# First batch's attention in two halves of its query rows, with layer 1 of the first 256 tokens between them

## The chip, the cores and the metric

The kernel runs on one core of a Trainium2 chip. A time is the device time of one execution in microseconds (us). Engines: TensorE (PE, its weight loads PEld), VectorE (DVE), ScalarE (ACT), GpSimd (POOL), and SyncE (SP), whose queue issues nearly all DMAs here. Each engine takes its instructions in the order of the program and waits at one that is not ready.

## What is computed

Inputs and outputs are float32 (the layer 1 to 3 weights float64). Attention with a block-causal mask over 8 batches, 8 heads, 576 tokens and head size 64, a gated double layer, and a top-1 mixture of 8 experts:

```python
scores = scale * np.matmul(q, k.transpose(0, 1, 3, 2))
mask = (pos[:, None] // 64) >= (pos[None, :] // 64)
attn = softmax(np.where(mask, scores, -1e9))
x = np.matmul(attn, v)               # to (4608 tokens, 512)
h = ((x @ w1) * (x @ w2)) @ w3       # 512 -> 1024 -> 1024
x2 = h @ w_out                       # 1024 -> 512
# gate logits of x2, one expert of 8 per token, relu(x2 @ w1[e]) @ w2[e], times the gate
```

## The kernel before

Nearly all matmuls are made of a high and a low float32r part of each operand (`split`: ACT writes the high part as a copy, DVE or POOL the low part as a subtraction), so that three matmuls, or two where one operand's parts are stacked, give one float32 product.

**Attention** (`attention`, a generator) goes through 32 pairs of heads, four pairs to a batch, nine steps to a pair. A step is a tile of 128 query rows: (hd, i) is head hd, rows 128 i onwards, with 128 (i + 1) key columns; (0, 4) is the last 64 rows of both heads. A step's stages are in successive iterations: scores on PE, one later the row maximum on DVE (L288), two later the exponential on ACT (L296), three later the normalization by DVE and POOL (L303), five later the transposes on PE, six later their evacuation by ACT and DVE to `pth` and `ptl`, seven later the product with V on PE (L350), eight later its output and split into `xph` and `xpl`. While a pair is in work the next one's inputs are prepared: ACT writes the high parts of q, K and V (L178, L189, L199), POOL the low parts (L183, L194, L204). The raw tiles are single buffers, so a load waits on SP until both engines have read the one before.

**The float32 route.** For pairs 0 to 2 (`N_RAW`) q and K are not split: `score_f32` multiplies them as float32, at four passes of PE.

**Layer 1** (`layer1(b)`) multiplies batch b's 576 tokens with w1 and w2: 8 feature blocks, 2 halves of 288 tokens, 2 weights, 12 matmuls each, so 384 matmuls a batch. It can start when all four pairs of the batch are through, that is 8 iterations behind the pair's last step.

**The weight decoder** (`decoder`) turns 16 chunks of float64 words of w1 and w2 into parts: for each chunk two copies on ACT (L113, L104), three integer instructions on DVE (L120, L121, L123), one subtraction on POOL (L105). Twelve chunks go ahead of layer 1, four beside it.

**The order** comes from one loop: attention yields after each half iteration, and `filler` (decoder, then layer 1 of batches 0 to 6) is advanced by a debt, 600 ns of estimated work a yield until batch 0 is ready, then 2335 ns an iteration less the attention's own PE cost. Behind attention come layer 1 of the last batch, the fold of w3 with w_out, routing and the experts.

Of the kernel before, what the change touches and what calls it, by code (L numbers as in the profile page):

```python
# [19 lines left out]

N_RAW, N_DEC = 3, 12
# [25 lines left out]
def tile_moe_stack(ctx: ExitStack, tc: tile.TileContext, qd, kd, vd, w1, w2, w3t, wo, wg,  # L47
                   e1, e2, c_id, c_msk, c_tri, c_row, c_cst, out):
    nc = tc.nc
# [97 lines left out]

    def attention(sa):
# [12 lines left out]
        def load(p, what):  # L161
            if p >= NP:
                return
            shape, src = {"q": ([128, 2, 640], qd), "k": ([128, 2, 576], kd), "v": ([128, 5, 2, 64], vd)}[what]
# [6 lines left out]
            raws[p, what] = t = raw.tile(shape, F32, tag=what + "r", name=what + "r")  # L171
            nc.sync.dma_start(out=t, in_=src[p])

        def prep_q1(p, h):
            if h == 0:
                ops.setdefault(p, {})
                ops[p]["X"] = opd.tile([128, 2, 640], F32R, tag="X", name="X")
            nc.scalar.activation(out=ops[p]["X"][:, h], in_=raws[p, "q"][:, h], func=AF.Copy)  # L178

        def prep_q2(p, h):  # L180
            q_, x = raws[p, "q"], ops[p]["X"]
            os_ = slice(64 - 64 * h, 128 - 64 * h)
            nc.gpsimd.tensor_tensor(out=x[os_, h], in0=q_[os_, h], in1=x.bitcast(F32)[os_, h],  # L183
                                                          op=ALU.subtract)

        def prep_k1(p, h):
            if h == 0:
                ops[p]["K1"] = opd.tile([128, 2, 576], F32R, tag="K1", name="K1")
            nc.scalar.activation(out=ops[p]["K1"][:, h], in_=raws[p, "k"][:, h], func=AF.Copy)  # L189

        def prep_k2(p, e):

            ops[p]["K2", e] = t = opd.tile([128, 576], F32R, tag="K2", name="K2", bufs=3)
            nc.gpsimd.tensor_tensor(out=t, in0=raws[p, "k"][:, e], in1=ops[p]["K1"].bitcast(F32)[:, e], op=ALU.subtract)  # L194

        def prep_v1(p):
            vv = opd.tile([128, 5, 2, 128], F32R, tag="VV", name="VV")
            ops.setdefault(p, {})
            nc.scalar.activation(out=vv[:, :, :, 0:64], in_=raws[p, "v"], func=AF.Copy)  # L199
            ops[p]["VV"] = vv  # L200

        def prep_v2(p):
            vv, v_ = ops[p]["VV"], raws[p, "v"]
            nc.gpsimd.tensor_tensor(out=vv[:, :, :, 64:128], in0=v_, in1=vv.bitcast(F32)[:, :, :, 0:64],  # L204
                                    op=ALU.subtract)

        def split_only(f):
            def go(p):
                if p >= N_RAW:
                    f(p)  # L210
            return go

        def then(f, what):
            def go(p):
                f(p)
                if what == "v" or p >= N_RAW:
                    load(p + 1, what)
            return go

        def early(p):  # L220
            if p + 1 < N_RAW:
                load(p + 1, "q")
                load(p + 1, "k")

        def first_split(p):
            if p == N_RAW - 2:
                load(N_RAW, "q")
                load(N_RAW, "k")

        prep_at = [(0, 0, then(prep_v2, "v")), (0, 1, split_only(lambda p: prep_q1(p, 0))),  # L230
                   (1, 1, split_only(lambda p: prep_q2(p, 0))), (1, 1, split_only(lambda p: prep_q1(p, 1))),
                   (2, 1, then(split_only(lambda p: prep_q2(p, 1)), "q")), (3, 1, split_only(lambda p: prep_k1(p, 0))),
                   (4, 1, split_only(lambda p: prep_k2(p, 0))), (4, 1, split_only(lambda p: prep_k1(p, 1))),
                   (6, 1, then(split_only(lambda p: prep_k2(p, 1)), "k")), (8, 1, prep_v1)]

        def score_f32(n, p, hd, i):
            X, K = ops[p]["X"].bitcast(F32), ops[p]["K1"].bitcast(F32)
            if i < 4:
                w_ = 128 * (i + 1)
                st = ps_s.tile([128, 512], F32, tag="s", name="s")  # L240
                nc.tensor.matmul(st[:, :w_], lhsT=X[0:64, hd, 128 * i:128 * i + 128], rhs=K[0:64, hd, :w_], start=True, stop=True)
                jobs[n] = dict(parts=[(st[:, :w_], 0, w_)], n=w_)
                return 4 * w_ / 2.4
            parts = []
            for c in range(2):
                st = ps_s.tile([128, 512], F32, tag="s", name="s")
                sl = slice(288 * c, 288 * c + 288)
                for h in range(2):
                    nc.tensor.matmul(st[:, :288], lhsT=X[0:64, h, 512:640], rhs=K[0:64, h, sl], start=(h == 0), stop=(h == 1))
# [863 lines left out]
```

## Time and profile before

| | |
|---|---|
| three runs | 1587.75 us median, 1581.91 to 1590.41 |
| profiled execution | 1582.65 us, span 1580.9 us |
| busy PE, DVE, ACT, POOL | 1516.8, 976.9, 883.8, 744.0 us |
| instructions | 28995 |

Busy time is the time in which an engine has an instruction in work; on PE matmuls overlap, so the start to start distance of two of them is what a matmul costs. In a timeline row the bracket at the end is the engine's idle time before the instruction and what ended it. In a group row the number behind the comma is the mean duration of one in ns.

### The profile page before, as it was taken

To read this page: it belongs to the slowest core of one execution; us is meant where nothing else is said; L and a number is where in the kernel's file an instruction comes from. 1 tells how busy PE (TensorE), PEld (TensorE's weight loads), DVE (VectorE), ACT (ScalarE), POOL (GpSimd) and SP (SyncE) were. 2 spreads that over 40 slices of the span, in tenths; PEclk is the share of its full clock that TensorE was granted. 3 is DMA by queue.
4 is the path that set the end of the run, shared out by engine and by line. 5 is a ranking of instruction groups with operands and counts; after the bars stand their busy time and mean duration, and the time that the engine had idled before them with its cause. 6 is when DMAs were issued, how large, how long until landed. Compare 5 with 4: busy or idle time off the path is not lost. (4 is left out here: it accounts for less than half of the span.)

```text
span 1580.9 us, 28995 instructions
## 1 busy us (share of the span) xinstructions
PE 1516.8 (96%) x10715; PEld 1422.6 (90%) x10715; DVE 976.9 (62%) x2546; ACT 883.8 (56%) x1961; POOL 744.0 (47%) x727
## 2 busy tenths in 40 slices
PE   6988999999999999999999999996999999999998
PEld 3568999999999999999999999995998898888897
DVE  6888666666666666666569243354655665566652
ACT  5696666677666677666434333322645555455542
POOL 4587655656566565654224001001536544645532
PEclk9999999999999999999999999997999999999999
DMA  6533232232323223230563556625166525455330
GB/s 181 146 110 96 91 103 88 87 103 88 104 94 102 89 86 103 89 94 24 158 188 104 143 138 151 139 62 173 57 224 236 180 74 208 163 219 194 139 141 28
DMA packets 56739, 197.61 MB, mean 125 GB/s; under 512 B 8656, under 2 KB 9040, under 8 KB 53010
## 3 DMA queue, kind: packets, MB, share of 16 engines
q1 hardware_dynamic: 44306, 117.29, 25.7%
q0 software_dynamic: 12288, 78.42, 13.9%
q8 instruction: 87, 1.43, 0.4%
q14 instruction: 58, 0.48, 0.1%
HBM read 187.26 MB, written 38.56 MB: 143 GB/s over the span
## 5 line engine op out<-in xcount | busy, mean ns | idle before, releaser
L303 POOL TENSOR_SCALAR P<-P,m 128x512 f32<-128x512 f32 (+4 forms) x288 | 161.7, 562 | 216.4 <-DVE m L302 159.9
L73 DVE TENSOR_TENSOR wl<-wr,wh 128x1024 fp32r<-128x1024 f32 x128 | 214.4, 1700 | 71.0 <-ACT wh L72 70.9
L770 PE MATMUL hps<-xhl,wh 128*128 128x256 f32 x1152 | 207.8, 283 | 0.8 <-ACT xhl L751 0.7
L813 PE MATMUL yps<-wh,hhw 128*128 128x512 f32 x624 | 201.3, 398 | 3.7 <-DVE hhw L775 2.7
L288 DVE CUSTOM_DVE_ANT_0 P<-s,msk 128x512 f32<-128x512 f32 (+2 forms) x320 | 152.1, 483 | 77.1 <-PE t L320 45.4
L72 ACT ACTIVATE wh<-wr 128x1024 fp32r<-128x1024 f32 x168 | 169.7, 1061 | 31.5 <-DMA wr<-e,widx 31.5
L770 PEld LDWEIGHTS hps<-xhl,wh 128*128 128x128 f32 x1152 | 179.9, 190 | 3.1 <-ACT xhl L751 1.1
L296 ACT ACTIVATE P<-P,m 128x512 f32<-128x512 f32 (+4 forms) x288 | 166.7, 579 | 11.1 <-DVE m L288 9.4
L307 DVE TENSOR_TENSOR ptl<-t,pth 128x512 fp32r<-128x512 f32 (+3 forms) x288 | 146.4, 508 | 38.4 <-ACT pth L306 33.0
L770 PE MATMUL hps<-xhl,wl 128*128 128x256 f32 x576 | 163.7, 284 | 4.3 <-POOL wl L73 4.3
L547 PE MATMUL x<-wfh,abh 128*128 128x264 f32 (+1 forms) x576 | 165.1, 287 | 0.0
L547 PE MATMUL x<-wfl,abh 128*128 128x264 f32 (+1 forms) x576 | 163.9, 285 | 0.0
L547 PE MATMUL x<-wfh,abl 128*128 128x264 f32 (+1 forms) x576 | 163.7, 284 | 0.0
L455 ACT ACTIVATE ab<-mm 128x288 f32<-128x288 f32 x128 | 52.6, 411 | 182.4 <-PE mm L449 181.3
L320 PE MATMUL t<-ident,P 128*128 128x128 f32 x768 | 136.3, 281 | 12.8 <-DVE m L301 12.8
L813 PEld LDWEIGHTS yps<-wh,hhw 128*128 128x128 f32 x624 | 116.8, 188 | 32.5 <-DVE hhw L775 5.6
L306 ACT ACTIVATE pth<-t 128x512 fp32r<-128x512 f32 (+3 forms) x288 | 129.0, 448 | 4.1 <-PE t L320 0.9
L350 PE MATMUL av<-ptl,VV 128*128 128x256 f32 (+1 forms) x448 | 125.6, 303 | 4.0 <-DVE m L301 3.5
L350 PE MATMUL av<-pth,VV 128*128 128x256 f32 (+1 forms) x448 | 126.9, 302 | 0.7 <-ACT pth L306 0.7
L813 PE MATMUL yps<-wl,hhw 128*128 128x512 f32 x312 | 122.8, 394 | 0.0
L775 DVE SCALAR_TENSOR_TENSOR hhw<-hps,hhw 128x512 fp32r<-128x512 f32 x72 | 49.7, 690 | 118.0 <-ACT hhw L774 117.7
L320 PEld LDWEIGHTS t<-ident,P 128*128 128x128 f32 x768 | 96.6, 143 | 27.6 <-issue 14.3
(224 smaller groups left out, 4444.6 us busy)
## 6 DMA issues: line engine op xcount, KB each, us to landing
qr<-qd SPq DMA_DIRECT2D x29, 640.0 KB, 4.5
abT<-ab SPq DMA_DIRECT2D x64, 288.0 KB, 4.6
abr<-abT SPq DMA_DIRECT2D x36, 512.0 KB, 10.4
kr<-kd SPq DMA_DIRECT2D x29, 576.0 KB, 3.9
vr<-vd SPq DMA_DIRECT2D x32, 320.0 KB, 2.9
str<-w SPq DMA_DIRECT2D x16, 512.0 KB, 4.3
str<-w3t SPq DMA_DIRECT2D x16, 512.0 KB, 3.7
x2d<-row SPq DMA_DIRECT2D x7, 1026.0 KB, 10.5
```

Source lines behind the costliest of these rows:

```text
L72: nc.scalar.activation(out=hi, in_=src, func=AF.Copy)
L73: (eng or nc.vector).tensor_tensor(out=lo, in0=src, in1=hi.bitcast(F32), op=ALU.subtract)
L288: nc.vector.tensor_tensor_reduce(out=pr[:, o_:o_ + w_], in0=s_, in1=msk[:, c_:c_ + w_], scale=-0.125, scalar=BIG, op0=ALU.add, op1=ALU.min ...
L296: nc.scalar.activation(out=pr, in_=pr, func=AF.Exp, bias=m[:, 0:1], scale=-1.0, accum_out=m[:, 3:4])
L303: nc.gpsimd.tensor_scalar(out=pr, in0=pr, scalar1=m[:, 6:7], scalar2=1.0, op0=ALU.mult, op1=ALU.mult)
L306: nc.scalar.activation(out=dst_h, in_=src, func=AF.Copy)
L307: nc.vector.tensor_tensor(out=dst_l, in0=src, in1=dst_h.bitcast(F32), op=ALU.subtract)
L320: nc.tensor.transpose(t_[:, 128 * c:128 * c + 128], pr[:, 128 * c:128 * c + 128], ident)
L350: nc.tensor.matmul(t_[:, x0:n], lhsT=vv[:, k_, hd, :], rhs=pt[:, hd, o_ + x0:o_ + n], start=(c == 0), stop=(c == 2 * kcs - 1))
L547: nc.tensor.matmul(ps[:, :c1 - c0], lhsT=u[:, k_, j * 128:j * 128 + 128], rhs=w_[:, k_, c0:c1], start=(c == 0), stop=(c == 23))
L770: nc.tensor.matmul(ps[:, d], lhsT=u[:, f2, k_, 128 * d:128 * d + 128], rhs=x[:, k_], start=(c == 0), stop=(c == 11))
L813: nc.tensor.matmul(ps, lhsT=u[:, g, o_], rhs=w_[:, g * 512:g * 512 + 512], start=(c == 0), stop=(c == 23))
```

## The change

Batch 0's attention is made of eight units instead of four pairs: first rows 0 to 255 of pairs 0 to 3 (part 0: 4 steps each, 256 key columns, 2 blocks of V), then rows 256 to 575 of pairs 0 to 3 (part 1: 5 steps each, all keys, so K and V are loaded and split once more). The other 28 pairs are units of nine steps as before; there are 288 steps in both kernels. Layer 1 of batch 0 goes in two calls, 256 tokens as soon as part 0 of all four pairs is through (step 15 plus 8 iterations), 320 tokens after part 1. All pairs are split; the float32 route is gone. One decoder runs through all 16 chunks, at a debt of 420 ns a yield, and is advanced beside layer 1's first half. The quota of an iteration is 1950 ns up to step 80. The K subtraction of the first unit is on DVE.

```diff
+    class Unit:
+        def __init__(self, p, part):
+            self.p, self.part = p, part
+            self.seq = {None: [(0, 4)] + [(hd, i) for hd in range(2) for i in (3, 2, 1, 0)],
+                        0: [(hd, i) for hd in range(2) for i in (1, 0)],
+                        1: [(0, 3), (0, 2), (0, 4), (1, 3), (1, 2)]}[part]
...
+            self.q0, self.q1 = (256 if part == 1 else 0), (256 if part == 0 else 640)
+            self.kw, self.vb = (256, 2) if part == 0 else (576, 5)
...
-            if p < N_RAW and what != "v":
-                nm = {"q": "X", "k": "K1"}[what]
-                t = opd.tile(shape, F32R, tag=nm, name=nm)
-                ops.setdefault(p, {})[nm] = t
-                nc.sync.dma_start(out=t.bitcast(F32)[0:64], in_=src[p, 0:64])
-                return
...
+            (nc.gpsimd if u else nc.vector).tensor_tensor(out=t[:, :kw], in0=raws[u, "k"][:, e],
+                                                          in1=ops[u]["K1"].bitcast(F32)[:, e, :kw], op=ALU.subtract)
...
+        v_at = {}
+        for u in range(len(units)):
+            v_at.setdefault(max(start[u] - 1, start[u - 1] + L_AV - 1 if u > 1 else 0, 0), []).append(u)
...
-        def score_f32(n, p, hd, i):
...
+        load(0, "q")
+        load(0, "k")
         nc.sync.dma_start(out=msk, in_=c_msk)
         nc.sync.dma_start(out=ident, in_=c_id)
+        load(0, "v")
         yield -1, 0
...
+        for _, _, f in prep_at:
+            f(0)
...
-    NP = 4 * B
-    seq = [(0, 4)] + [(hd, i) for hd in range(2) for i in (3, 2, 1, 0)]
+    units = [Unit(p, part) for part in range(2) for p in range(4)] + [Unit(p, None) for p in range(4, 4 * B)]
+    steps = [(u, j) for u, a in enumerate(units) for j in range(len(a.seq))]
...
-                for c in decoder(pool(wst, "wst", 1), ch[:N_DEC], nraw=3):
-                    yield c
...
+                dec = decoder(pool(wst, "wst", 1), ch, nraw=3)
...
+                while (0, 0) not in ready:
+                    yield -1 if tick() is None else 1550
+                def before(f_):
+                    while ticks < (11 if f_ < 4 else 20):
+                        tick()
+                l1 = layer1(0, ((0, 256),), before)
...
+            yield from l1
+            yield from wait((0, 1))
+            yield from layer1(0, ((256, 576),))
...
-            debt += 600 if 0 not in ready else (2335 if n < NP * NJ - 9 else 2000) / 2 - cost
+            if (0, 0) not in ready:
+                debt += 420
+            else:
+                debt += (1950 if n < 80 else 2335 if n < len(steps) - 9 else 2000) / 2 - cost
```

What the change does to the order is shown at three places. The first is the start of SP's queue; `qr`, `kr`, `vr` are the raw tiles of q, K and V, `X` and `K` in the kernel before are tiles that the float32 route reads as they land, `c_tri` is a constant, `str` the raw weights. Before:

```order
L169 DMA X<-qd 64x1280
L169 DMA K_124<-kd 64x1152
L172 DMA vr<-vd 128x640
L381 DMA msk<-c_msk 128x512
L382 DMA ident<-c_id 128x128
L90 DMA str<-w 128x1024 x2
L385 DMA t_131<-c_tri 128x256
```

and with the change:

```order
L186 DMA qr<-qd 128x2x256
L186 DMA kr<-kd 128x2x256
L365 DMA msk<-c_msk 128x512
L366 DMA ident<-c_id 128x128
L186 DMA vr<-vd 128x256
L88 DMA str<-w 128x1024 x2
L186 DMA qr<-qd 128x2x256
L186 DMA kr<-kd 128x2x256
L376 DMA t_158<-c_tri 128x256
```

The loads of the second unit's q and K now stand ahead of `c_tri`, whose reader on ACT (tile `tri`, L396 before, L382 now) stands ahead of the first exponential in both.

The second place is POOL's queue in the middle of batch 0's attention, where weight chunks are decoded (`w20l` is the low part of a chunk, `P` a step's normalization, `VV`, `X` and `K` low parts of V, q and K). Before, behind the first chunk of w2:

```order
L105 TENSOR_TENSOR w20l<-stw,w20h 128x512
L303 TENSOR_SCALAR P<-P,m 128x512
L303 TENSOR_SCALAR P<-P,m 128x384
L105 TENSOR_TENSOR w20l<-stw,w20h 128x512
L204 TENSOR_TENSOR VV<-vr,VV 128x10x64
L303 TENSOR_SCALAR P<-P,m 128x256
L105 TENSOR_TENSOR w20l<-stw,w20h 128x512
```

and with the change:

```order
L103 TENSOR_TENSOR w20l<-stw,w20h 128x512
L71 TENSOR_TENSOR xpl<-xf,xph 128x256
L219 TENSOR_TENSOR VV<-vr,VV 128x4x64
L286 TENSOR_SCALAR P<-P,m 128x128
L198 TENSOR_TENSOR X<-qr,X 64x384 x2
L103 TENSOR_TENSOR w20l<-stw,w20h 128x512
L286 TENSOR_SCALAR P<-P,m 128x256
L209 TENSOR_TENSOR K_496<-kr,K_494 128x576
L286 TENSOR_SCALAR P<-P,m 128x128
L209 TENSOR_TENSOR K_518<-kr,K_494 128x576
L103 TENSOR_TENSOR w20l<-stw,w20h 128x512
```

Low parts of q and K now stand between the chunks. The third place is on PE, where layer 1 of batch 0 (reads `xph`) ends and that of batch 1 (reads `xqh`) starts. Before:

```order
L266 MATMUL s<-K_4801,X 128x256
L267 MATMUL s<-K_4920,X 128x256
L320 MATMUL t<-ident,P 128x128 x3
L449 MATMUL mm<-xqh,w10h 128x288
L449 MATMUL mm<-xql,w10h 128x288
L449 MATMUL mm<-xqh,w10l 128x288
```

and with the change:

```order
L439 MATMUL mm<-xph,w21h 128x288
L439 MATMUL mm<-xpl,w21h 128x288
L439 MATMUL mm<-xph,w21l 128x288
L307 MATMUL t<-ident,P 128x128 x3
L439 MATMUL mm<-xqh,w10h 128x288
L439 MATMUL mm<-xql,w10h 128x288
L439 MATMUL mm<-xqh,w10l 128x288
```

Layer 1 of batch 0 ends a few instructions later in the order than before; from the three transposes on, the rest of PE's program is the same in both kernels.

## Rows read from the trace of the kernel before

**Rows 1.** the page, share of PE, and POOL's normalization, mean ns behind the bar

```profile
PE 1516.8 (96%) x10715; PEld 1422.6 (90%) x10715; DVE 976.9 (62%) x2546; ACT 883.8 (56%) x1961; POOL 744.0 (47%) x727
...
L303 POOL TENSOR_SCALAR P<-P,m 128x512 f32<-128x512 f32 (+4 forms) x288 | 161.7, 562 | 216.4 <-DVE m L302 159.9
```

**Rows 2.** windows: stretch, length, busy PE, PEld, DVE, ACT, POOL, clock, DMA share, GB/s

```profile
0.00:60.00 60.00, 46.25 (x110) 25.90 (x111) 47.42 (x112) 32.63 (x75) 30.19 (x38) 1.00 0.64 181
...
60.00:112.00 52.00, 43.98 (x231) 32.82 (x229) 40.33 (x162) 42.90 (x116) 41.26 (x48) 1.00 0.33 101
...
80.00:112.00 32.00, 26.26 (x166) 21.37 (x166) 27.55 (x111) 30.42 (x84) 28.97 (x34) 1.00 0.31 100
...
200.00:300.00 100.00, 99.28 (x750) 97.81 (x749) 65.21 (x243) 69.38 (x186) 58.56 (x68) 1.00 0.33 98
```

**Rows 3.** timeline of PE, first 210 us: start us, busy us, instruction

```profile
6.55 4.18 PE L249 MATMUL s<-K,X 64*128 64x288 f32 x8 [6.55 <-DMA K<-kd]
...
69.30 0.47 PE L350 MATMUL av<-ptl,VV 128*128 128x320 f32 x1
69.56 0.47 PE L350 MATMUL av<-pth,VV 128*128 128x320 f32 x1
...
112.80 0.38 PE L449 MATMUL mm<-xph,w10h 128*128 128x288 f32 x1
113.01 0.29 PE L449 MATMUL mm<-xpl,w10h 128*128 128x288 f32 x1
113.14 0.30 PE L449 MATMUL mm<-xph,w10l 128*128 128x288 f32 x1
...
209.99 0.38 PE L449 MATMUL mm<-xqh,w10h 128*128 128x288 f32 x1
```

**Rows 4.** timeline of ACT: first exponential of pairs 0, 4, 6 and 7

```profile
12.29 0.77 ACT L296 ACTIVATE P<-P,m 128x576 f32<-128x576 f32 x1
...
103.48 0.78 ACT L296 ACTIVATE P<-P,m 128x576 f32<-128x576 f32 x1
...
151.40 0.77 ACT L296 ACTIVATE P<-P,m 128x576 f32<-128x576 f32 x1
...
174.22 0.77 ACT L296 ACTIVATE P<-P,m 128x576 f32<-128x576 f32 x1
```

**Rows 5.** groups by shape, POOL, 300 to 392.4 us: busy us, mean ns

```profile
L183 POOL TENSOR_TENSOR X<-qr,X 64x640 fp32r<-64x640 f32 x8 | 12.5, 1563 | 0.3
...
L194 POOL TENSOR_TENSOR K<-kr,K 128x576 fp32r<-128x576 f32 x8 | 11.5, 1436 | 0.0
...
L73 POOL TENSOR_TENSOR xql<-xf,xqh 128x320 fp32r<-128x320 f32 x3 | 2.6, 881 | 3.2 <-ACT xqh L72 3.2
...
L73 POOL TENSOR_TENSOR xql<-xf,xqh 128x256 fp32r<-128x256 f32 x3 | 2.2, 735 | 2.9 <-ACT xqh L72 2.9
```

**Rows 6.** timelines of POOL and of DVE, 116 to 136 us, weight decoder

```profile
119.63 1.72 POOL L105 TENSOR_TENSOR w21l<-stw,w21h 128x512 fp32r<-128x512 f32 x1
...
130.29 1.45 POOL L105 TENSOR_TENSOR w21l<-stw,w21h 128x512 fp32r<-128x512 f32 x1
...
133.76 1.30 POOL L105 TENSOR_TENSOR w21l<-stw,w21h 128x512 fp32r<-128x512 f32 x1 [2.02 <-ACT w21h L104]
...
118.78 0.42 DVE L120 TENSOR_SCALAR stw<-stw 128x512 int32<-128x512 int32 x1
...
120.23 1.66 DVE L123 SCALAR_TENSOR_TENSOR stw<-str,stw 128x512 int32<-128x512 int32 x1
...
132.32 0.69 DVE L123 SCALAR_TENSOR_TENSOR stw<-str,stw 128x512 int32<-128x512 int32 x1
```

**Rows 7.** timelines of SP and ACT at the start, and the page's DMA issues

```profile
4.52 0.43 SPq L385 DMA_DIRECT2D t<-c_tri  x1
...
10.86 0.42 ACT L396 ACTIVATE tri<-t 128x256 bf16<-128x256 f32 x1 [3.10 <-DMA t<-c_tri]
...
vr<-vd SPq DMA_DIRECT2D x32, 320.0 KB, 2.9
```

More of the change, by code (lines that the diff above doesn't have):

```diff
@@ L174, in prep_q1 @@
-        def prep_q1(p, h):
-            if h == 0:
[L176 to L181, printed above, removed]
+            t = raw.tile(shape, F32, tag=what + "r", name=what + "r")
+            if what == "v":
+                t, src = t[:, :a.vb], src[a.p, :, :a.vb]
+            else:
+                c0, c1 = (a.q0, a.q1) if what == "q" else (0, a.kw)
+                t, src = t[:, :, c0:c1], src[a.p, :, :, c0:c1]
@@ L205, in prep_v2 @@
+        def prep_v2(u):
+            vv = ops[u]["VV"][:, :units[u].vb]
+            nc.gpsimd.tensor_tensor(out=vv[:, :, :, 64:128], in0=raws[u, "v"], in1=vv.bitcast(F32)[:, :, :, 0:64],
                                     op=ALU.subtract)
[L207 to L210, printed above, removed]
-            return go
[L213 to L218, printed above, removed]
@@ L236, in score_f32 @@
-        def score_f32(n, p, hd, i):
[L237 to L249, printed above, removed]
-                parts.append((st[:, :288], 288 * c, 288))
-            jobs[n] = dict(parts=parts, n=576)
-            return 1920
@@ L871, in experts @@
                     run(s, s + 1)
-    NP = 4 * B
-    seq = [(0, 4)] + [(hd, i) for hd in range(2) for i in (3, 2, 1, 0)]
-    NJ = len(seq)
+    units = [Unit(p, part) for part in range(2) for p in range(4)] + [Unit(p, None) for p in range(4, 4 * B)]
+    steps = [(u, j) for u, a in enumerate(units) for j in range(len(a.seq))]
+    start = [steps.index((u, 0)) for u in range(len(units))]
     NW3 = 4
@@ L899, in filler, with wait, tick @@
                         ch.append((src[k_ * 128:k_ * 128 + 128, cs], wts[nm, c][0][:, k_], wts[nm, c][1][:, k_], None))
+            tp = pool(sq, "tp", 2)
+            def wait(*parts):
+                while not all(p in ready for p in parts):
+                    yield -1
             with ExitStack() as wst:
[L901 to L909 removed]
+                dec = decoder(pool(wst, "wst", 1), ch, nraw=3)
+                ticks = 0
+                def tick():
+                    nonlocal ticks
+                    ticks += 1
+                    return next(dec, None)
+                yield tick()
+                while (0, 0) not in ready:
[3 more added lines that the diff above has]
+                        tick()
+                debt = 0
+                l1 = layer1(0, ((0, 256),), before)
                 for c in l1:
@@ L912, in filler @@
                     debt += c
-                    left = True
-                    while debt > 0 and left:
-                        left = next(dec, None) is not None
+                    while debt > 0:
+                        tick()
                         debt -= 1400
-                    if not left:
+                    if ticks >= 20:
                         break
-                for _ in dec:
-                    pass
             qq = pool(sq, "xqq", 1)
```

211 lines of the change are left out of this document (102 added, 109 removed).

## The prediction

> **What bounds the kernel now.** I read the page first, then the windows, then the timeline of the first 210 us. TensorE (PE) is busy for 1516.8 of 1580.9 us [rows 1]. The windows show where the rest is: from 200 us on PE is busy 99.28 of 100 us, in the first 60 us only 46.25, and from 60 to 112 us 43.98 of 52 [rows 2]. So the change can act only ahead of about 200 us.
>
> A busy PE of that stretch is not a fast one. Two matmuls of 320 columns start 0.26 us apart at 69.56 us, which is 1.2 GHz; layer 1's, with 288 columns, start 0.13 us apart at 113 us, which is 2.4 GHz, though the granted clock stands at 1.00 in both windows [rows 2, 3]. What paces the start is the other engines: VectorE (DVE) with 47.42 of 60 us while it decodes weights, then ScalarE (ACT) with 42.90 and GpSimd (POOL) with 41.26 of 52 us [rows 2].
>
> The marks that I use: the exponential of step 0 starts at 12.29 us, that of step 36 (first step of pair 4) at 103.48 us [rows 4]; the first layer 1 matmul at 112.80 us; the first layer 1 matmul of batch 1 at 209.99 us [rows 3]. I call the last one the join. The order shows that behind it PE's instructions are the same in both kernels, row for row. The profiled execution took 1582.65 us, so 1372.7 us lie behind the join in either kernel, and the change is worth what it moves the join.
>
> **What the change adds and removes before step 36.** It pulls layer 1 of tokens 0 to 255 ahead: by the order 72 of its 192 matmuls stand on PE before step 36, at 0.12 us each (256 columns by the 0.13 us of 288) 8.6 us of PE work that was behind it. It removes the float32 scores of pairs 0 to 2. They cost PE only, in a stretch in which PE had room; I count nothing for it, and the cover is POOL's work below.
>
> In exchange pairs 0 to 2 must now be split like the others, the first 256 columns of K and two blocks of V are split twice, and all 16 weight chunks are decoded by then instead of 12. Most of that lands on POOL, so I add POOL up. Step 36's inputs need:
> - 36 normalizations, 0.562 us each [rows 1]: 20.2 us, as before.
> - Second parts of q: 8 of 256 columns, 8 of 384, where before there were 2 of 640. The 640 takes 1.563 us; the same operation with 256 columns takes 0.735 us; for 384 I take 1.0 [rows 5]. 13.9 us.
> - Second parts of K: 6 of 256 (the first two go to DVE), 8 of 576 at 1.436 us [rows 5]: 15.9 us.
> - Second parts of V: 4 of 256 columns, 4 of 640, taken as q's: 9.2 us.
> - Splits of the attention output: 4 at 0.735, 4 at 0.881 us [rows 5]: 6.5 us.
> - 16 weight chunks at 1.30 us [rows 6]: 20.8 us, before 12.
> - Pair 4's own inputs, 3 x 1.563 + 2 x 1.436 = 7.6 us.
>
> The sum is 94.0 us. The same list for the kernel before (36 normalizations, 8 output splits, q and K of pairs 3 and 4 alone, 5 full V, 12 chunks) gives 62.1 us. POOL had 32 us less to do by step 36, and even so it was a busy engine from 80 to 112 us: 28.97 us of 32 [rows 2].
>
> **The decoder and POOL stand in each other's way.** POOL's weight subtraction took 1.30 us alone at 133.76 us, and 1.72 us at 119.63 us while DVE ran a decoder instruction; DVE's took 0.69 us at 132.32 us with POOL idle, 1.66 us at 120.23 us [rows 6]. From 119.63 us to the end of the subtraction that starts at 130.29 us POOL did not pause: 12.11 us for three chunks, three 640 column splits and three normalizations, which alone take 3 x 1.30 + 3 x 1.563 + 3 x 0.562 = 10.28 us. So a chunk costs POOL 0.61 us more; for the 15 chunks behind the first that is 9.2 us. Bounds: nothing, if DVE slips into POOL's gaps, and 1.8 us a chunk, all of DVE's three decoder instructions (0.42 + 0.69 + 0.69 us [rows 6]), 27 us.
> The Trainium skill (SBUF — State Buffer, section Who interferes with whom) says that a VectorE instruction with two SBUF inputs and a GpSimd instruction that reads SBUF exclude each other for the whole instruction. By that rule the upper bound would hold and step 36 come 18 us later still. The trace agrees that they exclude each other (1.66 us against 0.69), but shows 0.61 us a chunk.
>
> **The start.** The order moves the constant load c_tri on SyncE's (SP's) queue behind the loads of the second unit's q and K, which reuse the first unit's only raw buffers. First inputs were in at 6.55 us [rows 3]; four conversions of 0.42 us (c_tri's own, of 256 columns [rows 7]) and two subtractions of 0.735 us free the buffer near 8.5 us, two issues later c_tri starts at about 9.8 instead of 4.52 us [rows 7] and lands, with the 2.9 us of a V load at the least and the 6.3 us that it took before (4.52 to 10.86 us) at the most, between 12.7 and 16 us. ACT stands in front of it: I take 13 us. Between it and the first exponential ACT then has c_tri's conversion and seven others of 256 or 512 columns, eight of 0.42 us or somewhat more, 3.9 us: 17 us instead of 12.29. Queued behind ACT are DVE's first decoder instructions and with them its normalizations, and behind those POOL. Right behind the second exponential ACT needs the second unit's V, whose load waits on SP until POOL has split the first V (near 17.8 us); with its issue and 2.9 us [rows 7] it lands at 21.3 us, and POOL's first weight chunk, which comes after it on ACT, ends near 22 us. Bounds: 19 us, if the V is there in time, and 25 us, if c_tri takes its 6.3 us. By then POOL has 7.0 of its 94.0 us behind it.
>
> **The sum.** Left for POOL: 87.0 + 9.2 = 96.2 us from 22 us on. Without a pause step 36 comes at 118.2 us; with the 90.5% that POOL reached from 80 to 112 us, at 128.3 us. DVE, which paces the decoding now, has as many weights as before in its 47.42 us and four more, so it gives POOL little slack; I take 125 us, against 103.48.
>
> From step 36 to the join PE is the bound in the new kernel: 44 steps of attention and 384 - 72 = 312 layer 1 matmuls of 0.13 us. A pair with its 96 matmuls takes 22.82 us (151.40 to 174.22 us [rows 4]), 12.5 of them layer 1, so nine steps of attention are 10.3 us. 44 x 10.3 / 9 + 312 x 0.13 = 91 us; with PE's small waits I take 93.5. The join comes at 218.5 us, 8.5 us late. Own time 1582.65 + 8.5 = 1591 us; the median of the runs shown, 1587.75 us, lies 5.1 us above the profiled one, so I forecast 1596 us. With 0.5% (7.9 us, about the spread of the three runs and what can be told from no change) the decision is at step 36: before 108.6 us the kernel is faster, after 124.4 us slower.
>
> **Other edits.** ACT gets 32 more conversions by step 36, at 0.42 us and somewhat more each, some 15 us: POOL's 32 us more hide them, and without that cover step 36 would be 15 us late by ACT alone. Eight more abT stores and four more K loads are SP work that nobody reads before the next stage. The lower quota of filler (1950 instead of 2335 before step 80) only shares out PE's time; by the order layer 1 of batch 0 ends right before the join in both kernels, so nothing is left over.
>
> **The rivals.**
> - POOL and DVE interleave without loss, and the start costs less (19 us): step 36 at 19 + 87.0 = 106 us, the join at 199.5, 10.5 us early: 1577 us. For it: from 80 to 112 us POOL ran at 90.5% with DVE at 27.55 of 32 us beside it [rows 2]. Against it: no decoder ran there, and [rows 6]. It decides if step 36 comes before 108.6 us. Chance 0.29, of which 0.24 beyond 0.5%.
> - The change does not move the end: step 36 comes 13 us late, near 116 us, with the port's lower bound and the start as I have it plus a few small pauses (22 + 87.0 / 0.93), and PE wins the 13 us back behind it (106.5 us from 103.48 to 209.99 before, 93.5 after); 1587 us. Chance 0.10.
> - Lock step: with 1.8 us a chunk on POOL and 90.5% busy step 36 comes at 22 + (87.0 + 27) / 0.905 = 148 us, halfway at 139, the join at 232 to 241: 1610 to 1619 us. PE adds to this if its clock, still at 1.2 GHz at 69.56 us, stays there into layer 1: 72 matmuls at twice 0.12 us are 8.6 us more. Chance 0.11.
> - The forecast, step 36 between 119 and 135 us, 1590 to 1606 us: chance 0.50, 0.30 of it beyond 0.5%.
>
> **Numbers.** Faster 0.24. Same 0.05 + 0.10 + 0.20 = 0.35. Slower 0.30 + 0.11 = 0.41. The range reaches to the first rival and past the forecast's end: 1575 to 1612 us. The likeliest case's own range is 1590 to 1606 us.
>
> **What would show it.** In the new profile: the first exponential near 17 us and ACT waiting for c_tri; POOL over 90% busy from 22 us to about 120 us, with DVE's decoder instructions of 1.6 us beside it; layer 1 starting near 85 us; step 36 near 125 us; the join near 218 us and 1373 us behind it. Wrong if POOL shows pauses yet step 36 comes before 110 us (my POOL sum is too long), or if PE is not full between step 36 and the join.

## The result, and the profile after

The changed kernel takes 1605.84 us (median of 4 runs, 1598.08 to 1606.97), beside 1588.37 us for the kernel before (median of 4 runs): a ratio of 1.0104, interval 1.0067 to 1.0141. It is about 1% slower. The profiled execution took 1598.08 us.

The page, line of PE, answers to [rows 1]; PE has 18 us less to do and the kernel is longer all the same:

```profile
PE 1499.0 (94%) x10715; PEld 1423.4 (89%) x10715; DVE 996.6 (62%) x2548; ACT 895.9 (56%) x1993; POOL 771.2 (48%) x757
```

The windows answer to [rows 2], with one more from the prediction's 22 us to step 36 (stretch, length, busy PE, PEld, DVE, ACT, POOL, clock, DMA share, GB/s):

```profile
0.00:60.00 60.00, 22.46 (x73) 16.81 (x74) 44.70 (x102) 31.69 (x91) 39.05 (x55) 1.00 0.59 179
60.00:112.00 52.00, 34.91 (x171) 29.82 (x170) 50.70 (x108) 35.91 (x85) 41.81 (x40) 0.90 0.41 132
...
200.00:300.00 100.00, 100.00 (x748) 98.27 (x748) 67.92 (x263) 72.70 (x197) 63.98 (x75) 1.00 0.31 100
...
22.00:136.00 114.00, 70.80 (x354) 60.66 (x355) 105.33 (x242) 75.04 (x188) 90.17 (x92) 0.94 0.44 137
```

Behind 200 us nothing is new: PE is full. Ahead of it PE has lost half of its work of the first 60 us (22.46 instead of 46.25), and DVE has risen from 40.33 to 50.70 of the 52 us behind 60 us. The engine that fills the slow stretch is DVE, with 105.33 of 114 us, not POOL with 90.17.

The timeline of PE (start us, busy us, instruction) answers to [rows 3]: the first layer 1 matmul, the join, and a third mark, the last layer 1 matmul of all, which stands at 822.30 us in the kernel before.

```profile
84.08 0.36 PE L439 MATMUL mm<-xph,w10h 128*128 128x256 f32 x1
...
230.04 0.30 PE L439 MATMUL mm<-xqh,w10h 128*128 128x288 f32 x1
...
840.14 0.30 PE L439 MATMUL mm<-xqh,w21l 128*128 128x288 f32 x1
```

The timeline of ACT answers to [rows 4, 7]: c_tri's conversion, the first exponential, and step 36's.

```profile
12.45 0.42 ACT L382 ACTIVATE tri<-t 128x256 bf16<-128x256 f32 x1 [6.96 <-DMA t<-c_tri]
...
15.40 0.50 ACT L279 ACTIVATE P<-P,m 128x256 f32<-128x256 f32 x1
...
135.79 0.76 ACT L279 ACTIVATE P<-P,m 128x576 f32<-128x576 f32 x1
```

So the loss grows to 32.3 us at step 36 (135.79 against 103.48), shrinks to 20.05 at the join and is 17.84 at the last layer 1 matmul. What lies behind that matmul takes 757.9 us here and 760.3 in the kernel before. In those kernels below that decode the weights it takes 758 to 762 us too, so this mark tells their profiled time to about 2 us (e2 and e12, which leave the decoding out, take 752.4 and 754.1 us).

Where DVE's time went, by form, first the changed kernel from 6 to 136 us (busy us, mean ns, then idle before):

```profile
L119 DVE SCALAR_TENSOR_TENSOR stw<-str,stw 128x512 int32<-128x512 int32 x16 | 21.6, 1351 | 0.6
L121 DVE SCALAR_TENSOR_TENSOR stw<-str,stw 128x512 int32<-128x512 int32 x16 | 18.2, 1140 | 0.5
L118 DVE TENSOR_SCALAR stw<-stw 128x512 int32<-128x512 int32 x16 | 17.2, 1073 | 6.0 <-ACT stw L111 6.0
L274 DVE TENSOR_TENSOR m<-m 128x1 f32<-128x1 f32 x5 | 8.7, 1731 | 0.2
```

The same view of the kernel before, from 6 to 104 us, also up to step 36:

```profile
L123 DVE SCALAR_TENSOR_TENSOR stw<-str,stw 128x512 int32<-128x512 int32 x12 | 11.2, 930 | 0.4
L121 DVE SCALAR_TENSOR_TENSOR stw<-str,stw 128x512 int32<-128x512 int32 x12 | 10.9, 908 | 0.4
L120 DVE TENSOR_SCALAR stw<-stw 128x512 int32<-128x512 int32 x12 | 9.4, 785 | 0.4 <-ACT stw L113 0.4
```

A weight chunk costs DVE 57.0 / 16 = 3.6 us now, 31.5 / 12 = 2.6 us before, and 0.42 + 0.69 + 0.69 = 1.8 us undisturbed [rows 6]. For 16 chunks that is 28 us of waiting that counts as busy. L274 is the oddest line: the minimum of two columns of 128x1 takes 1.73 us on average. The five are far from alike: two take 0.16 us, two 1.16 us and one 6.02 us. The timelines of DVE and of POOL around the longest:

```profile
86.10 6.02 DVE L274 TENSOR_TENSOR m<-m 128x1 f32<-128x1 f32 x1
92.04 0.27 DVE L290 TENSOR_TENSOR ptl<-s,pth 64x128 fp32r<-64x128 f32 x1
...
85.89 1.42 POOL L209 TENSOR_TENSOR K<-kr,K 128x576 fp32r<-128x576 f32 x1
87.28 1.56 POOL L219 TENSOR_TENSOR VV<-vr,VV 128x640 fp32r<-128x640 f32 x1
88.83 0.68 POOL L286 TENSOR_SCALAR P<-P,m 128x512 f32<-128x512 f32 x1
89.49 1.39 POOL L209 TENSOR_TENSOR K<-kr,K 128x576 fp32r<-128x576 f32 x1
90.84 1.25 POOL L103 TENSOR_TENSOR w11l<-stw,w11h 128x512 fp32r<-128x512 f32 x1
```

The minimum reads two SBUF operands. It begins 0.21 us after a POOL instruction and ends at 92.12 us, just when POOL's run of five comes to its end at 92.09 us. The four POOL instructions that start behind it all went first. A decoder instruction fared alike: L118, begun at 50.82 us, lasted 5.06 us, until 0.29 us after a run of POOL had ended at 55.59 us. But a run isn't always waited out. At 106.31 us a minimum met the same two POOL instructions, K and then VV without a pause, and got in between them:

```profile
106.31 1.16 DVE L274 TENSOR_TENSOR m<-m 128x1 f32<-128x1 f32 x1
...
106.03 1.42 POOL L209 TENSOR_TENSOR K<-kr,K 128x576 fp32r<-128x576 f32 x1
107.42 1.80 POOL L219 TENSOR_TENSOR VV<-vr,VV 128x640 fp32r<-128x640 f32 x1
```

What decides between the two stays open. In sum the waiting is lopsided: up to step 36 DVE waits some 36 us in the decoder and the minima, while POOL's own instructions take some 7 us longer than without the exclusion (e12 below). POOL's idle time comes largely of this in turn: of its 23.8 us from 22 to 136 us, 17.5 stand in front of its normalizations, 14.4 of them for DVE's reciprocals (L285), which are queued behind a waiting DVE. Two of the five forms, from the groups by form of POOL in that window:

```profile
L286 POOL TENSOR_SCALAR P<-P,m 128x512 f32<-128x512 f32 x8 | 6.3, 789 | 5.0 <-DVE m L285 3.3 <-ACT P L279 1.5
...
L286 POOL TENSOR_SCALAR P<-P,m 128x384 f32<-128x384 f32 x8 | 5.3, 660 | 3.1 <-DVE m L285 3.0
```

### The profile page after: what moved, and what is told of

It reads as the page before. It is cut to its first block, busy times and chain, and to the rows that moved or that the text cites. A ratio compares the mean times of both kernels' runs of the same rounds, so it can differ in the third digit from the quotient of the medians.

```text
span 1596.2 us, 29166 instructions
## 1 busy us (share of the span) xinstructions
PE 1499.0 (94%) x10715; PEld 1423.4 (89%) x10715; DVE 996.6 (62%) x2548; ACT 895.9 (56%) x1993; POOL 771.2 (48%) x757
## 3 DMA queue, kind: packets, MB, share of 16 engines
q0 software_dynamic: 12288, 78.42, 13.7%
## 5 line engine op out<-in xcount | busy, mean ns | idle before, releaser
L286 POOL TENSOR_SCALAR P<-P,m 128x384 f32<-128x384 f32 (+4 forms) x288 | 162.5, 565 | 191.7 <-DVE m L285 126.4
L271 DVE CUSTOM_DVE_ANT_0 P<-s,msk 128x256 f32<-128x256 f32 (+2 forms) x320 | 151.9, 482 | 55.8 <-PE t L307 37.8
L279 ACT ACTIVATE P<-P,m 128x384 f32<-128x384 f32 (+4 forms) x288 | 166.9, 580 | 29.0 <-DVE m L271 16.8
L445 ACT ACTIVATE ab<-mm 128x288 f32<-128x288 f32 (+2 forms) x128 | 52.5, 410 | 157.6 <-PE mm L439 156.9
L696 POOL DMA_INDIRECT wr<-e,widx x42 | 46.7, 1112 | 158.6 <-issue 65.8
## 6 DMA issues: line engine op xcount, KB each, us to landing
abr<-abT SPq DMA_DIRECT2D x36, 512.0 KB, 10.8
```

The costliest lines, as they stand in the source:

```text
L271: nc.vector.tensor_tensor_reduce(out=pr[:, o_:o_ + w_], in0=s_, in1=msk[:, c_:c_ + w_], scale=-0.125, scalar=BIG, op0=ALU.add, op1=ALU.min ...
L279: nc.scalar.activation(out=pr, in_=pr, func=AF.Exp, bias=m[:, 0:1], scale=-1.0, accum_out=m[:, 3:4])
L286: nc.gpsimd.tensor_scalar(out=pr, in0=pr, scalar1=m[:, 6:7], scalar2=1.0, op0=ALU.mult, op1=ALU.mult)
```

## The experiments

Marks of the profiled executions, in us; "last L1" is the last layer 1 matmul. In e6 and e11 layer 1 is shared out otherwise, and 82 steps' exponentials lie ahead of the join instead of 78 or 79, so their join is no mark. Medians are of all runs of a kernel. Each ratio is to runs of the kernel before made beside it, whose median lay between 1585 and 1588 us, so two kernels are compared better by their ratios than by their medians.

| kernel | first exp | step 36 | join | last L1 | median | ratio (interval) |
|---|---|---|---|---|---|---|
| before | 12.29 | 103.48 | 209.99 | 822.30 | 1585 to 1588 | |
| changed | 15.40 | 135.79 | 230.04 | 840.14 | 1605.84 | 1.0104 (1.0067 to 1.0141) |
| e1 constants first | 15.69 | 137.6 | 231.88 | 841.98 | 1601.70 | 1.0094 (1.0065 to 1.0123) |
| e2 one-input decoder | 16.0 | 116.30 | 210.62 | 820.73 | 1573.14 | one run |
| e12 and minimum | 16.6 | 109.39 | 201.88 | 811.92 | 1566.02 | one run |
| e5 minimum alone | 16.2 | 137.2 | 229.67 | 839.66 | 1600.40 | 1.0095 (1.0062 to 1.0129) |
| e3 before, no raw route | 15.1 | 114.8 | 222.86 | 835.15 | 1591.47 | 1.0036 (1.0019 to 1.0054) |
| e7 halves, no mixing | 16.3 | 134.8 | 239.20 | 851.56 | 1612.09 | 1.0175 (1.0142 to 1.0208) |
| e4 mixing, old quotas | 16.1 | 140.6 | 234.75 | 847.06 | 1605.57 | 1.0115 (1.0083 to 1.0147) |
| e6 raw route kept | 13.8 | 121.2 | (226.24) | 826.75 | 1589.37 | 1.0041 (1.0021 to 1.0062) |
| e11 raw route, leaner | 15.0 | 123.6 | (227.36) | 827.50 | 1585.99 | 1.0007 (0.9992 to 1.0023) |
| e10 norms on ACT | 16.04 | 146.53 | 240.88 | 851.10 | 1610.27 | 1.0149 (1.0122 to 1.0176) |
| e8 leaner before | 12.2 | 101.98 | 208.13 | 818.83 | 1578.94 | 0.9966 (0.9949 to 0.9983) |
| e9 and norms on ACT | 12.26 | 114.17 | 221.72 | 832.54 | 1588.42 | 1.0016 (0.9998 to 1.0033) |

One execution's marks and the median don't always agree to better than some 6 us (e3: 12.9 us at the last L1, 5 in the medians), so a gap of less than that in a single mark proves little.

**e1: the start.**

```diff
-        for _, _, f in prep_at:
-            f(0)
         t2 = pp.tile([128, 576], F32, tag="P", name="t2")[:, 0:256]
         ti = pp.tile([128, 576], F32, tag="P", name="ti")[0:1, 0:RW]
         for dst_, src in ((t2, c_tri), (cst, c_cst)):
             nc.sync.dma_start(out=dst_, in_=src)
+        for _, _, f in prep_at:
+            f(0)
```

> The changed kernel with the loads of c_tri and the gate constants moved back ahead of the loads of the second unit's q and K. Theory (VectorE is busy 84 to 98% of every 10 us from 20 us on, so it paces the way to step 36, and what it starts earlier it ends earlier): ScalarE's wait for c_tri falls from 6.96 to about 3 us, the first exponential comes near 12.5 us instead of 15.40, step 36 near 133 and the join near 227 instead of 230.04 us; the time falls by about 3 us. Rival (a later stage, such as the sharing of TensorE between attention and layer 1, sets step 36, and the start is absorbed): the first exponential moves and step 36 stays within 1 us of 135.8, the join within 1 us of 230.0.

The load was issued 2.9 us earlier and landed no earlier. Timelines of SP and ACT of e1:

```profile
4.63 0.43 SPq L374 DMA_DIRECT2D t<-c_tri  x1
...
12.74 0.42 ACT L382 ACTIVATE tri<-t 128x256 bf16<-128x256 f32 x1 [7.31 <-DMA t<-c_tri]
```

In the changed kernel it was issued at 7.51 us and its conversion began at 12.45. Neither theory had that: the issue's place on SP is not what sets the arrival, so the first exponential did not move, and whether the start is absorbed could not be tried this way. What sets the arrival stays open; in the kernel before c_tri, issued at 4.52 us, was converted at 10.86 [rows 7].

**e2 and e12: the exclusion taken away.** e2 replaces the decoder's three DVE instructions by reductions of about their length, so the weights are not decoded; e12 replaces the minimum (the line of e5) as well.

```diff
-                wi = val[b_].bitcast(I32)
-                nc.vector.tensor_scalar(out=wi, in0=wi, scalar1=3, scalar2=None, op0=ALU.logical_shift_left)
-                nc.vector.scalar_tensor_tensor(out=wi, in0=r[:, :, 0], scalar=29, in1=wi,
-                                               op0=ALU.logical_shift_right, op1=ALU.bitwise_or)
-                nc.vector.scalar_tensor_tensor(out=wi, in0=r[:, :, 1], scalar=-2 ** 31, in1=wi,
-                                               op0=ALU.bitwise_and, op1=ALU.bitwise_or)
+                for z in range(3):
+                    nc.vector.tensor_reduce(out=val[b_][:, z:z + 1], in_=val[b_][:, 8:512], axis=AX.X, op=ALU.max)
```

> The changed kernel with the decoder's three VectorE instructions on a chunk replaced by three reductions over the same tile, which read one SBUF input each and last about as long as the decoder's do alone (some 1.8 us a chunk). The weights are then not decoded, so only the marks up to the join are compared. Theory (the decoder's two-input instructions and GpSimd's stand in each other's way on both sides; VectorE spends 3.6 us on a chunk that alone takes 1.8, some 29 us for 16 chunks, and that is what the prediction left out): VectorE's decoder time falls to 1.8 to 2.2 us a chunk, step 36 comes at 108 to 118 instead of 135.8 us, the join at 202 to 212. Rival A (GpSimd's own sum of 94 us decides, as the prediction had it): step 36 no earlier than 120 us, the join no earlier than 214. Rival B (the number of VectorE instructions and their queueing, not the exclusion, is what costs): reductions last as long as the decoder's did, step 36 stays at 130 us or later.

> The changed kernel with both of VectorE's kinds of instruction that stand in GpSimd's way replaced: three one-input reductions for the decoder's instructions, as before (step 36 at 116.3 us), and the minimum as a reduction, so that the 11.6 us of five minima up to step 36 go as well. The weights are not decoded; only marks up to the join and the last matmul of layer 1 are compared. Theory (GpSimd's holding time is what is left of VectorE's loss): step 36 at 106 to 112 us, near the 106 us of the prediction's rival without exclusion, and GpSimd over 90% busy up to there. Rival (from 70 us on TensorE and the chain of a step pace the mixed stretch, not VectorE): step 36 at 114 to 117 us.

Step 36 came at 116.30 us, and with the minimum gone too at 109.39 us: with these instructions replaced it comes 26.4 us earlier (one execution), beside a delay of 32.3 us. That is about what the exclusion costs the changed kernel there. It is not all excess over the kernel before, whose own decoder waits 31.5 - 12 x 1.8 = 9.9 us by the rows above, and which was not run without the exclusion. In e2 the waits had moved to the five minima (11.6 us up to step 36), which is why e12 was needed. In e12, by form, from 6 to 110 us, the reductions last what they take undisturbed, and the window from 22 to 109 us has POOL as the full engine:

```profile
L118 DVE TENSOR_REDUCE stw<-stw 128x1 f32<-128x504 f32 x48 | 29.5, 669 | 7.2 <-ACT stw L111 7.2
...
22.00:109.00 87.00, 64.84 (x349) 55.26 (x350) 72.07 (x242) 74.61 (x191) 83.24 (x93) 0.92 0.55 182
```

DVE spent 29.5 us on the reductions and would have needed 16 x 1.8 = 28.8 us for the decoder alone, so it is the waiting and not less work that makes the difference. The reductions also leave the raw weights unread; but in the changed kernel no engine's idle time up to step 36 ended with the landing of raw weights, so earlier loads of them explain little. POOL's 83.24 us in 87 us refute the rival of e12 (TensorE or the chain of a step).

**e5: one wait taken away alone.**

```diff
-                nc.vector.tensor_tensor(out=m[:, 0:1], in0=m[:, 0:1], in1=m[:, 1:2], op=ALU.min)
+                nc.vector.tensor_reduce(out=m[:, 0:1], in_=m[:, 0:2], axis=AX.X, op=ALU.min)
```

> The changed kernel with one word of VectorE's work changed: the minimum of the two partial maxima of a 576 column row, an instruction on 128x1 with two SBUF inputs, becomes a reduction over 128x2 with one SBUF input. Theory (an instruction with two SBUF inputs waits on VectorE until GpSimd's instruction ends, whatever its own size; the five up to step 36 last 1.73 us each, 8.7 us): the five last 0.1 to 0.3 us each, VectorE has some 7 us less to do up to step 36, which comes at 128 to 132 instead of 135.8 us; the join at 222 to 227 instead of 230.04; the time 3 to 8 us shorter. Rival (the wait only moves on to the next decoder instruction, since GpSimd holds the port as long as before): the decoder's three instructions grow by as much, step 36 stays within 1.5 us of 135.8 and the join within 1.5 us of 230.0.

The rival held. By form, DVE from 6 to 138 us:

```profile
L118 DVE TENSOR_SCALAR stw<-stw 128x512 int32<-128x512 int32 x16 | 22.5, 1406 | 7.0 <-ACT stw L111 7.0
L119 DVE SCALAR_TENSOR_TENSOR stw<-str,stw 128x512 int32<-128x512 int32 x16 | 21.6, 1352 | 0.6
L121 DVE SCALAR_TENSOR_TENSOR stw<-str,stw 128x512 int32<-128x512 int32 x16 | 18.2, 1139 | 0.5
...
L274 DVE TENSOR_REDUCE m<-m 128x1 f32<-128x2 f32 x5 | 0.8, 155 | 0.2
```

The minima fell from 8.7 to 0.8 us, and L118 rose from 17.2 to 22.5 us, so 5.3 of the 7.9 us moved on to it; step 36 (1.4 us later) and the join (0.4 us earlier) stayed within the rival's 1.5 us. The wait belongs to POOL's run of work more than to the instruction that happens to meet it.

**e3, e7, e4: the change put together piece by piece.** e3 is the kernel before with

```diff
-N_RAW, N_DEC = 3, 12
+N_RAW, N_DEC = 0, 12
```

> The kernel before with the float32 route of pairs 0 to 2 alone taken away: these pairs are split like the others, there are no half units, 12 chunks are decoded at the start as before, and layer 1 is not pulled ahead. It tells which part of the change costs. Theory (the splits of pairs 0 to 2 put some 20 us of work on GpSimd that stretch VectorE's two-input instructions beside them): step 36 comes 12 to 18 us later than the 103.48 of the kernel before, the join 8 to 16 us later than 209.99, and the time is 8 to 16 us longer. Rival (the half units and the four chunks more are what costs; the float32 scores took as much TensorE time as the splits take elsewhere): step 36 within 5 us of 103.48, the time within 4 us of the kernel before.

e7 is the changed kernel with

```diff
-                while (0, 0) not in ready:
+                while (0, 1) not in ready:
...
-                l1 = layer1(0, ((0, 256),), before)
+                l1 = layer1(0, before=before)
```

(without the second call for the other columns, and with the quotas 600 and 2335).

> The changed kernel without the mixing: half units as in the change, no raw route, but layer 1 of batch 0 starts when both halves are there, as one piece, with the quotas of the kernel before. It stands between the kernel before without its raw route (step 36 at 114.8, join at 222.9 us) and the changed one. Theory (what costs is GpSimd's and VectorE's work before step 36; the halves add 8 K and 4 V splits of 256 columns, 9 us on GpSimd and their waits on VectorE; mixing pays back little of it): step 36 at 121 to 130 us, the join at 228 to 234. Rival (the halves cost nothing by themselves, and the pulled-ahead layer 1 and its four chunks of weights are what costs): step 36 at 113 to 118, the join at 221 to 226 us.

e4 is the changed kernel with these quotas alone:

```diff
-                debt += 420
+                debt += 600
...
-                debt += (1950 if n < 80 else 2335 if n < len(steps) - 9 else 2000) / 2 - cost
+                debt += (2335 if n < len(steps) - 9 else 2000) / 2 - cost
```

> The changed kernel with the quotas of filler work of the kernel before: 600 instead of 420 before layer 1 is ready, 2335 instead of 1950 before step 80. Theory (VectorE paces the way to step 36, and layer 1's matmuls only fill TensorE's gaps): step 36 comes later by what more layer 1 is put ahead of it (1 to 4 us), the join moves by less than 3 us, the time by less than 3 us. Rival (the quotas hold attention back or starve TensorE, so they are what costs): the join moves by more than 5 us.

From e3 to e7 to e4 to the changed kernel, the last layer 1 matmul moves step by step: no raw route +12.9 us, half units (with all 16 chunks in the one decoder) +16.4, mixing -4.5, new quotas -6.9, together +17.8. e3's rival fell, and its theory held for the join (12.9 us later), but not quite at step 36 (11.3 us, short of its 12 to 18) and not in time: the median is 5.2 us longer than that of the kernel before beside it, short of 8 to 16. e7 cost more than its theory said (step 36 at 134.8 instead of 121 to 130, the join at 239.20 instead of 228 to 234), and its rival fell. By the ratios the half units are the dearest piece too (1.0036 to 1.0175). e4 fell between its theory and its rival: its quotas bring step 36 4.8 us later, a little over the theory's 1 to 4, and the join 4.7 us, between under 3 and over 5; the last L1 comes 6.9 us later, but the median equals the changed kernel's, so the quotas' worth stays unclear. The part that was to win, the mixing, seems to win: 4.5 us at the last L1, less than a single mark can prove, and a ratio of 1.0115 instead of 1.0175, with intervals that just overlap. At that mark it pays for about a quarter of what the half units cost.

**e6 and e11: the dearest removable piece undone.** e6 keeps the float32 scores of pairs 0 to 2 in half units:

```diff
+        def is_raw(u):
+            return units[u].part is not None and units[u].p < 3
...
+            if is_raw(u):
+                return score_f32(n, u, hd, i)
```

> The changed kernel with the float32 route for the scores of pairs 0 to 2 kept, in half units: it undoes that part of the change alone. Theory (each split on GpSimd costs twice, by its own time and by the time that it holds up VectorE's two-input instructions; without the raw route the kernel before lost 11.3 us at step 36 and 12.9 us at the join): VectorE's decoder falls from 3.6 to 2.6 to 3.0 us a chunk, step 36 comes at 118 to 126 instead of 135.8 us, the join at 212 to 220 instead of 230.04, the time 8 to 16 us shorter. Rival (mixing layer 1 into the stretch makes TensorE the bound there, so that float32 scores of four passes now cost what the splits did): step 36 within 4 us of 135.8.

> The changed kernel with the float32 route of pairs 0 to 2 kept (last layer 1 matmul at 826.75 us) and with the two VectorE savings of the leaner kernel before (minimum as a reduction, no addition of 1e-9). It is the best form of the change that the runs point to. Theory (the savings are worth what they were in the kernel before, 3.5 us at the last layer 1 matmul): that matmul at 821 to 825 us, the time 1580 to 1588 us, so not better than the leaner kernel before (818.83 and 1578.94 us), since half units still split K and V twice. Rival (with the float32 route in, VectorE's own work is what holds the stage up, and in half units each saving counts more): the last layer 1 matmul before 818 us and the time below 1578 us.

e6 came as its theory said at step 36 (121.2, 14.6 us earlier), in the decoder (47.0 / 16 = 2.9 us a chunk) and, by the ratios, in time (1.0104 to 1.0041, some 10 us; 16.5 us in the medians); its rival fell. Its join missed the 212 to 220 us, but is no mark here. e11's savings brought nothing at the last L1 (827.50 instead of 821 to 825); its time lies in the theory's range (1585.99), and its rival fell. This best form of the change that was run is level with the kernel before.

**e10, e8, e9: less for POOL to hold, less for DVE to do.** e10 moves the first 34 normalizations of the changed kernel, e9 the first 18 of e8's, from POOL to ACT:

```diff
-            nc.gpsimd.tensor_scalar(out=pr, in0=pr, scalar1=m[:, 6:7], scalar2=1.0, op0=ALU.mult, op1=ALU.mult)
+            if n < 34:
+                nc.scalar.activation(out=pr, in_=pr, func=AF.Copy, scale=m[:, 6:7])
+            else:
+                nc.gpsimd.tensor_scalar(out=pr, in0=pr, scalar1=m[:, 6:7], scalar2=1.0, op0=ALU.mult, op1=ALU.mult)
```

e8 is the kernel before with the line of e5 and without the addition of 1e-9:

```diff
-            nc.vector.tensor_scalar(out=m[:, 5:6], in0=m[:, 3:4], scalar1=1e-9, scalar2=None, op0=ALU.add)
-            nc.vector.reciprocal(out=m[:, 6:7], in_=m[:, 5:6])
+            nc.vector.reciprocal(out=m[:, 6:7], in_=m[:, 3:4])
```

> The changed kernel with the normalizations of its first 34 steps on ScalarE instead of GpSimd. VectorE's own work is the same. Theory (what VectorE loses is GpSimd's holding time; of its some 88 us from 15 to 136 us the normalizations are 20, and VectorE lost (3.6 - 1.8) x 16 + 7 = 36 us): VectorE's decoder and minimum together fall by 6 to 10 us, step 36 comes at 126 to 131 instead of 135.8 us, the last layer 1 matmul at 831 to 836 instead of 840.14. Rival A (only GpSimd's two-input instructions lock, the normalizations, with one, do not): VectorE's decoder stays at 3.5 us a chunk or more, step 36 within 2 us of 135.8. Rival B (ScalarE takes over as the engine that paces): the decoder falls, but ScalarE is over 90% busy and step 36 comes no earlier.

> The kernel before with two VectorE instructions made cheaper or left out: the minimum of two partial maxima as a reduction with one SBUF input, and no addition of 1e-9 to the sum of a softmax row (the sum holds exp(0) = 1, to which a float32 cannot add 1e-9). 142 ns a step, 5.1 us for 36 steps. Theory (VectorE, 85 to 97% busy from 10 to 60 us, paces the start of the kernel before too): step 36 comes at 98 to 101 instead of 103.48 us, the join at 205 to 208, the time 2 to 5 us shorter. Rival (up to step 36 ScalarE or GpSimd sets the pace, so VectorE's gain lands in its idle time): step 36 within 1 us of 103.5, the time within 1 us.

> The leaner version of the kernel before (last layer 1 matmul at 818.83 us, step 36 at 102.0) with the normalization of its first 18 steps, which fall into the decoding, on ScalarE instead of GpSimd. Theory (each instruction of GpSimd that reads SBUF holds up VectorE's decoder; the 18 are 9.5 of the some 30 us that GpSimd is busy from 10 to 66 us, in which the decoder loses 12 x 0.8 = 9.6 us): the decoder gets 2 to 3 us back, the last matmul of layer 1 comes at 815 to 817 us, the time 2 to 4 us below the leaner version's. Rival (ScalarE, some 60% busy there, stands in the chain of every step, and the 18 instructions of about 0.6 us delay exponentials and the decoder's conversions by more than the port gives back): step 18 and the last matmul 1 to 6 us later.

e10 did to DVE what the theory said, and more: up to step 36 the decoder fell from 57.0 to 48.0 us, 3.0 a chunk, which refutes rival A, and the minima from 8.7 to 4.3:

```profile
L121 DVE SCALAR_TENSOR_TENSOR stw<-str,stw 128x512 int32<-128x512 int32 x16 | 19.8, 1235 | 0.5
L119 DVE SCALAR_TENSOR_TENSOR stw<-str,stw 128x512 int32<-128x512 int32 x16 | 19.3, 1203 | 0.6
L118 DVE TENSOR_SCALAR stw<-stw 128x512 int32<-128x512 int32 x16 | 8.9, 558 | 6.8 <-ACT stw L111 6.8
L274 DVE TENSOR_TENSOR m<-m 128x1 f32<-128x1 f32 x5 | 4.3, 854 | 0.2
```

Yet step 36 came 10.7 us later. The window from 22 to 136 us, and the longest wait of any engine from 15 to 136 us (engine and line, waited for, us, times, longest):

```profile
22.00:136.00 114.00, 65.94 (x287) 52.96 (x288) 84.76 (x218) 84.15 (x208) 67.96 (x55) 0.91 0.41 130
...
ACT P L287 <- DVE m L285: 28.4, 20, 3.3
```

No engine is full any more (DVE 84.76, ACT 84.15 of 114 us). ACT now stands 28.4 us in front of normalizations whose sums DVE has not yet given, and what is queued behind them on ACT, the conversions that everybody else needs, waits too. That this order costs the 10.7 us is read from the waits; no run tests it alone. So a less busy DVE is not enough. Rival B had the outcome and the engine, but not the way: ACT is not over 90% busy, it waits in order. e9 is the same in the other kernel: step 36 comes 12.2 us and the last L1 13.7 us later than e8's, where its theory had a gain and its rival 1 to 6 us.

e8 is the version that beats both kernels: 1578.94 us, ratio 0.9966 (0.9949 to 0.9983). Step 36 came 1.5 us and the join 1.9 us earlier, between theory and rival, and the last L1 3.5 us: less than the 5.1 us that DVE was spared, more than nothing. The median is 6.2 us below that of the kernel before beside it, more than the theory's 2 to 5; where the rest comes from is not shown.

## Why the prediction was right, and where it was off

Direction and range held, but not the way to them. The forecast of 1596 us was 10 us short: 1605.84 lies at the very edge of the likeliest case's own range (1590 to 1606), and step 36, at 135.79 us, just outside that case's 119 to 135. Step 36 is 10.8 us later than forecast; the rest (0.8 us to the join, -4.6 behind it, 2.7 between the profiled execution and the median) nearly cancels. One sign failed: POOL was to be over 90% busy from 22 us on and had 90.17 of 114 us, 79%; the engine over 90% was DVE.

- The start: POOL's first chunk ended at 21.95 us (predicted 22), layer 1 began at 84.08 (85), the first exponential at 15.40 (17). The reason given for c_tri's lateness, its place on SP's queue, fell with e1.
- POOL's list: 87.0 us were left at 22 us; e12, without exclusion, shows 83.24 us, and step 36 at 109.39, where the list alone gives 22 + 87.0 = 109.0. The prices were right, the 1.0 us taken for a 384 column split among them (1000 ns in e12). That 109.0 meets 109.39 so well is in part luck: the list was 3.8 us too long (two of the output splits, 1.8 us, run only behind step 36), and POOL had 3.8 us of pauses.
- The exclusion on POOL's side: 9.2 us predicted; 90.17 - 83.24 = 6.9 us measured. Right in kind and nearly in size.
- The failed step is the term behind it, "DVE ... gives POOL little slack; I take 125 us". It left 125 - 22 - 96.2 = 6.8 us for POOL's pauses; they were 114 - 90.17 = 23.8 us. I priced the exclusion for POOL, from [rows 6], and left out its other side, although one of the four durations there was DVE's own 1.66 us instead of 0.69. DVE waited 28.2 us in the decoder and 7.9 us in the minima, stood at 105.33 of 114 us, and POOL waited for DVE's sums. 22 + 83.2 + 6.9 + 23.8 = 135.9 us is the measured step 36; the sum closes by construction, so what it shows is the size of each part. With the 3.8 us of pauses of e12 it would be 115.9 us, the prediction's own case of no change (116 us). So the direction hung on the pauses: the forecast took 6.8 us between its bounds of 0 and 10.1 us (118.2 and 128.3 us), and the real ones lie beyond both.
- The lock step rival had 139 to 148 us (by its own sum 138: 22 + (87.0 + 18.1) / 0.905). It charged POOL with DVE's instructions; in fact mostly DVE was charged with POOL's. The Trainium skill (SBUF — State Buffer, section Who interferes with whom) says that the loser waits for the whole instruction of the other. The 1.16 us of two minima agree with it; the 6.02 us of a third go beyond it: the loser waited for five.
- From step 36 to the join: 93.5 us predicted, 94.25 measured. Behind the join 1372.7 predicted, 1368.0 measured.
- The chance for a gain rested on POOL and DVE interleaving without loss; e12 shows that case (its join at 201.88 us, near the rival's 199.5), so it was a fair rival, and the exclusion is what decides against it.

Why removing work from PE did not pay: PE had room ahead of step 36. The float32 scores were its cheap way around POOL (step 36 came 11.3 us later without them in e3 and 14.6 us earlier with them in e6), and half units make POOL split the first columns of K twice.

## What to carry to other kernels

Where DVE and POOL both work in SBUF, price their exclusion on both sides: here it cost POOL some 7 us and DVE some 36. A small two-input instruction of DVE can wait for a whole run of POOL (6.02 us for a 128x1 minimum). Taking one such instruction away can move its wait to the next (5.3 of 7.9 us in e5), so count what DVE has left that POOL holds up. And read a busy share of DVE beside the durations of the same shapes elsewhere in the kernel, single ones and not only the mean, since such a wait counts as busy; where no engine is full and the stretch is still slow (e10), look for an engine that stands in order behind a late operand.

## What the runs showed of the hardware

- A one-input DVE instruction is not always free of POOL: L118 (128x512 int32, in place) takes 0.42 us alone and 1.41 us on average in e5. The reductions over the same tile kept to 0.669 us in e12.
- TensorE's clock fell after a wait: at 92.96 us PE had waited 4.14 us, and of the following 320 column matmuls two start 0.26 us apart (1.2 GHz). The granted clock is 1.00 from 88 to 90 us, 0.50 from 92 to 98 us and 1.00 again from 99 us; at 100.03 us they start 0.15 us apart (2.4 GHz). The timeline of PE of the changed kernel:

```profile
92.96 0.64 PE L337 MATMUL av<-ptl,VV 128*128 128x320 f32 x1 [4.14 <-DVE ptl L290]
93.40 0.47 PE L337 MATMUL av<-pth,VV 128*128 128x320 f32 x1
93.66 0.47 PE L337 MATMUL av<-ptl,VV 128*128 128x320 f32 x1
...
100.03 0.31 PE L337 MATMUL av<-ptl,VV 128*128 128x320 f32 x1
100.18 0.31 PE L337 MATMUL av<-pth,VV 128*128 128x320 f32 x1
```

The wait in front of it is the 6.02 us minimum again, since the DVE instruction that PE waits for stands behind it: a wait on DVE became a wait on PE and then a slower PE. What the slower stretch cost is not shown. The granted clock does not tell all: at 79.40 us two matmuls of 256 columns start 0.22 us apart, as slow, in a window granted 1.00.
